# Two transformer layer pairs on one core: x tiles loaded ahead of the weights, set-up behind the norm statistics, and a scheduler told the traced DMA landings

## The chip, the cores and the metric

The kernel runs on one NeuronCore of a Trainium2 chip. The core has a matrix engine (TensorE, "PE" in the profile; its weight loads are "PEld"), a vector engine (VectorE, "DVE"), an engine for activation functions (ScalarE, "ACT"), a general engine (GpSimd, "POOL"), and a queue that issues DMAs (SyncE, "SP"). The metric is the device time of one execution in microseconds (us), as the median of several runs.

## The reference

Four steps run in sequence on `x` of 2048 tokens by 512 features in bf16: attention, feed-forward, attention, feed-forward, with the same weights both times. In the kernel the attentions are called L = 1 and L = 3.

```python
def _A_ref(x, wqkv, wo):                       # 32 heads of 16 features
    qkv = (x @ wqkv).reshape(B, S, 3, 32, 16).transpose(2, 0, 3, 1, 4)
    scores = einsum("bhqd,bhkd->bhqk", q, k) * 16 ** -0.5
    o = einsum("bhqk,bhkd->bhqd", softmax(scores), v)
    return o.transpose(0, 2, 1, 3).reshape(B, S, 512) @ wo

def _B_ref(x, w1, b1, w2, b2):                 # 512 -> 1376 -> 512
    h = gelu(layernorm(x) @ w1 + b1)
    return h @ w2 + b2

x = x + _A_ref(layernorm(x), wqkv, wo)
x = x + _B_ref(layernorm(x), w1, b1, w2, b2)
x = x + _A_ref(layernorm(x), wqkv, wo)
x = x + _B_ref(layernorm(x), w1, b1, w2, b2)
```

## The kernel before

The kernel is written as jobs (Python generators) that hand tasks to a small list scheduler when the kernel is built. The scheduler keeps a modelled clock for each engine; each operation carries a duration `dur` and, for a DMA, a latency `lat` from the end of its issue to its landing. It picks the task that can start first, ties going to the lower priority number. What comes out is one fixed order of instructions for each engine, with semaphore waits; on the chip nothing is re-ordered. The modelled times therefore decide only the order.

A tile is 128 tokens, so x has 16 tiles. A chunk `qc` is four tiles of queries, a segment is one chunk and one group of four heads (`hg`). For each segment TensorE computes scores (L1240), the softmax exponential runs on ScalarE over two or three 128x512 tiles at once (L1225), and TensorE multiplies by V (L1409). Some of the key tiles (3, 6, 9, 12, 15) may take another way: VectorE makes an approximate exponential of them with integer operations (one L1317 each, and three L1348 for each pair). The first chunk of each layer is done in two parts: for L = 1, key tiles 0 to 3 first and 4 to 15 after them, so that attention starts before all keys exist.

How a DMA was booked before:

```python
op.t0 = max(self.free[eng], self.ready(eng, reads, writes, same_ok))
if eng == "sp":
    self.free[eng] = op.t0 + dur
    op.t1 = op.t0 + dur + (2.0 if lat is None else lat)
```

The start of the kernel (shortened; `now0` puts an instruction into its stream at once, ahead of all jobs):

```python
ldx(0, 1)
ldw(1, 512)          # K weights, 512 KB
ldx(1, 2)
ldx(2, 4)
ldw(0, 0)            # Q weights
ldw(2, 1024)         # V weights
self.S_.when([("ks", 1, 1)], lambda: ldx(4, 8))
self.S_.when([("ks", 1, 3)], lambda: ldx(8, 16))     # 1 MB in one DMA
...
dve = lambda fn, reads, writes, dur=0.2: n0("dve", I(fn, reads, writes, dur))
...
dve(memset zw) ; dve(memset of a PSUM bank) ; pads("dve", 2)
dve(memset of the ones column of V) ; dve(ident) ; dve(iogt) ; dve(row16) ; dve(onesm)
dve(qbias) ; dve(ioe) ; dve(mask8) ; dve(m4) ; dve(sel memset) ; dve(sel)     # L696 to L706
```

Then each of the first four tiles goes through its norm and its projections. Norm statistics are `bn_stats` and `bn_aggr` on VectorE (L808, L809) and two small operations on GpSimd (L816, L817); the normalised tile (L821) is transposed by DMA (L968) and multiplied by the K, Q and V weights (L989). Keys are transposed by DMA straight into the key buffer `KT` (L993), queries are stored to a scratch tensor (L1020) and read back, transposed, once for each segment:

```python
def flow_q(self):                                       # one transposed read per segment
    for sg in self.segs:
        ...                                             # the very first segment uses a PE transpose
        s = yield ("get", "qraw")                       # two buffers
        yield ("keys", [("qst", L, tt) for tt in sg["toks"]])
        yield self.dma(... dma_start_transpose(self.qraw[:, s:s + 1, 0:W], self.q_scr[...]) ...)   # L1074
        self.S_.spawn(self.job_qt(sg, s), ...)
```

For the second layer the keys and values of tiles 0 to 11 pass through scratch tensors, since the buffers are still in use by the first; each head group is reloaded when its last segment of L = 1 is done and all twelve tiles are stored:

```python
def job_kload(self, hg):
    yield ("keys", [(k, 3, tt) for k in ("ks", "vs") for tt in range(12)])
    yield self.dma(... dma_start_transpose(self.KT[:, hg:hg + 1, 0:1536], self.k_scr[...]) ...)     # L1109
    yield self.dma(... dma_start(self.V[:, hg, 0:12, ...], self.v_scr[...]) ...)                    # L1111
```

What follows attention (output projection, residual, norm, feed-forward, and for L = 1 the projections of the next layer) is one block per chunk, with a priority:

```python
def post_prio(self, L, qc):
    return 0.95 if (L, qc) == (1, self.NC - 1) else 1.6 if (L, qc) == (1, self.NC - 2) else 2.2
```

The products with V have priority 1.0, scores 0.0. While TensorE would idle, the scheduler inserts matmuls of zeros (L1150, L1153) to keep its clock up.

Of the kernel before, what the change touches and what calls it, by code (L numbers as in the profile page):

```python
# [62 lines left out]
class Prog:  # L63


    def __init__(self):
        self.streams = {e: [] for e in ENGINES}
        self.last_writer = {}
        self.readers = {}
        self.ops = []  # L70
        self.dma_rr = 0
        self.free = {e: 0.0 for e in ENGINES}
        self.tiling = "full"
        self.tiles = {}
        self.drain = 0.0
        self.work = []
# [25 lines left out]
    def op(self, eng, fn, reads=(), writes=(), same_ok=(), dur=0.3, lat=None):  # L102
# [10 lines left out]
        if eng == "sp":  # L113
            self.free[eng] = op.t0 + dur
            op.t1 = op.t0 + dur + (2.0 if lat is None else lat)
# [361 lines left out]
ACCB = 6  # L477
# [10 lines left out]
class Builder:  # L488
# [169 lines left out]
    def build_startup(self):  # L658
# [5 lines left out]
        def ldx(a, b):  # L664
            n0("sp", I(lambda e: e.dma_start(self.xres[:, a:b, :], xr[:, a:b, :]), writes=[("x", tt) for tt in range(a, b)], dur=0.1))

        def ldw(k, a):
            n0("sp", I(lambda e: e.dma_start(self.wqkv[:, :, a:a + 512], wr[:, :, a:a + 512]), writes=[("wqkv", k)], dur=0.1, lat=3.0))
        ldx(0, 1)
        ldw(1, 512)  # L670
        ldx(1, 2)
        ldx(2, 4)
        ldw(0, 0)
        ldw(2, 1024)
        self.S_.when([("ks", 1, 1)], lambda: ldx(4, 8))
        self.S_.when([("ks", 1, 3)], lambda: ldx(8, 16))

        pool = lambda fn, writes, dur=0.4, reads=(): n0("pool", I(fn, reads, writes, dur))
        dve = lambda fn, reads, writes, dur=0.2: n0("dve", I(fn, reads, writes, dur))
# [10 lines left out]
        dve(lambda e: e.memset(self.zw[:, :], 0.0), [], [("zw",)], 0.2)  # L690
        dve(lambda e: e.memset(self.ps[:, ACCB, :], 0.0), [], [("ps", ACCB)], 0.6)
# [3 lines left out]
        vv = self.V[:, :, :, :, :].rearrange("p g k h d -> p (g k h) d")  # L695
        dve(lambda e: e.memset(vv[:, :, 16:17], 1.0), [], [("V", hg, kb) for hg in range(8) for kb in range(16)], 0.7)  # L696
        dve(lambda e: e.tensor_scalar(out=self.ident[:, :], in0=self.ioi, scalar1=0.0, scalar2=None, op0=ALU.is_equal), [("ioi",)], [("ident",)], 0.25)
        dve(lambda e: e.tensor_scalar(out=self.iogt[:, :], in0=self.iog[:, :], scalar1=16.0, scalar2=None, op0=ALU.is_equal), [("iog",)], [("iogt",)])
        dve(lambda e: e.tensor_reduce(out=self.row16[:, :], in_=self.iogt[:, :], axis=AX.X, op=ALU.add), [("iogt",)], [("row16",)])
        dve(lambda e: e.tensor_scalar(out=self.onesm[:, :], in0=self.row16[:, :], scalar1=-1.0, scalar2=1.0, op0=ALU.mult, op1=ALU.add), [("row16",)], [("onesm",)])  # L700
        dve(lambda e: e.tensor_scalar(out=self.qbias[:, :], in0=self.row16[:, :], scalar1=OFFSET, scalar2=None, op0=ALU.mult), [("row16",)], [("qbias",)])
        dve(lambda e: e.tensor_scalar(out=self.ioe[:, :, :], in0=self.ioe[:, :, :], scalar1=0.0, scalar2=None, op0=ALU.is_equal), [("ioe",)], [("ioe",)])
        dve(lambda e: e.tensor_reduce(out=self.mask8[:, :], in_=self.ioe[:, :, :], axis=AX.X, op=ALU.add), [("ioe",)], [("mask8",)])
        dve(lambda e: e.tensor_reduce(out=self.m4[:, :], in_=self.ioe[:, :, :].rearrange("p g h -> p h g"), axis=AX.X, op=ALU.add), [("ioe",)], [("m4",)])
        dve(lambda e: e.memset(self.sel[:, :], 0.0), [], [("sel",)])
        dve(lambda e: e.tensor_copy(out=self.sel[:, :].rearrange("p (h c) -> p h c", c=32)[:, :, 16], in_=self.m4[:, :]), [("m4",)], [("sel",)])  # L706

    def build_startup_late(self):
# [4 lines left out]
        def fills():  # L713
# [18 lines left out]
            ld = lambda fn, reads, writes: self.dma(fn, reads, writes, 4.0, 0.45, 5.0)  # L732
# [30 lines left out]
    def flow_weights(self):  # L763
# [3 lines left out]
        ld = lambda fn, writes, dur, prio: self.dma(fn, [], writes, prio, dur, 3.5)  # L767
# [982 lines left out]
```

## Time and profile before

| what | before |
|---|---|
| device time | 1646.37 us, median of 3 runs (1645.89 to 1647.75) |
| span of the profiled run | 1641.4 us, granted TensorE clock 0.994 |
| first exponential of a segment (ScalarE) | at 26.2 us |
| start of the second part of the first chunk | at 95.2 us |
| last segment of L = 1 ends (VectorE reads its sum) | at 830.7 us |
| ScalarE busy, 26.23 to 95.16 us | 60.94 of 68.93 us |
| ScalarE busy, 1060 to 1245 us | 182.85 of 185 us |

The page gives busy time of each engine. In a list by time each line has a start, a length, the engine, the source line and operation, output and input, a count and, in brackets, how long the engine stood idle before it and what ended the wait. "issue" there means that the profile shows no reason. In a table of stretches each engine has its busy time, then come the TensorE clock as a share of full speed, the mean busy share of the 16 DMA engines and the GB/s moved. The chain of waits is followed back from the last instruction of the stretch asked about.

### The profile page before, as it was taken

The page shows a single profiled execution, that of the slowest core. Times are in us where ns is not written, and L with a number is a line of the kernel's source. Part 1 is how long each engine was busy: PE and PEld are TensorE (multiplying, and loading weights), DVE is VectorE, ACT ScalarE, POOL GpSimd, SP SyncE. Part 2 cuts the span into 40 slices and gives each one's busy share as a digit, 9 for nine tenths or more (in the row PEclk, how much of TensorE's full clock was granted, in tenths as well). Part 3 has the DMA queues.
Part 4 walks back from the last instruction along what each step waited for, and adds up shares of the span by engine and source line. Part 5 has one row for each costly group of instructions (what it writes and reads, how often), then busy time and mean ns, then how long its engine had stood idle before and what let it go on. Part 6 is the DMA issues. An engine that isn't in the chain of part 4 may idle for free.

```text
span 1641.4 us, 40475 instructions
## 1 busy us (share of the span) xinstructions
PE 1555.6 (95%) x16682; PEld 504.4 (31%) x16833; DVE 1481.7 (90%) x3255; ACT 1562.2 (95%) x1383; POOL 380.0 (23%) x575
## 2 busy tenths in 40 slices
PE   8989999999999999999999998999999999999998
PEld 4222222222222222222232222322222222344444
DVE  7789999998999899989979799999899989999894
ACT  5999999999999999999999999899999999999996
POOL 4355231111310112111121134511011101222220
PEclk9999999999999999999999999999999999999999
DMA  6562000202111121112281330000000100000000
GB/s 172 110 133 61 16 8 8 43 17 65 63 24 36 31 44 57 33 29 45 84 130 45 64 84 15 18 21 8 14 11 8 21 12 8 5 19 9 23 8 14
DMA packets 181238, 66.34 MB, mean 40 GB/s; under 512 B 160859, under 2 KB 175424, under 8 KB 181056
## 3 DMA queue, kind: packets, MB, share of 16 engines
q1 hardware_dynamic: 181056, 63.75, 17.4%
q8 instruction: 135, 2.21, 0.6%
q14 instruction: 47, 0.39, 0.1%
HBM read 19.96 MB, written 15.30 MB: 21 GB/s over the span
## 4 chain that ended last, share of the span: by engine, by line
PE 49%; DVE 24%; ACT 23%; issue 3%; DMA 1%; POOL 1%; DVEq 0%; SPq 0%
ACT PT L1225 21%; PE ps L1240 19%; PE ps L1409 14%; DVE dp L1317 9%; DVE dp L1348 7%; PE ps L1574 4%; PE ps L1536 4%; PE ps L876 3%; PE ps L1503 3%; PE ps L1150 2%; DVE accT L1439 1%; DVE OT L1479 1%; ACT h L1566 1%; DVE QT L1086 1%; DVE ob L1477 1%
## 5 line engine op out<-in xcount | busy, mean ns | idle before, releaser
L1225 ACT ACTIVATE PT<-ps 128x1024 bf16<-128x1024 f32 (+1 forms) x1304 | 1486.0, 1253 | 49.4 <-PE ps L1240 43.0
L1240 PE MATMUL ps<-QT,KT 32*128 32x512 bf16 (+1 forms) x4608 | 685.6, 359 | 44.0 <-DVE dp L1317 14.9
L1317 DVE TENSOR_SCALAR dp<-ps 128x512 uint16<-128x512 f32 x869 | 583.6, 679 | 76.8 <-PE ps L1240 72.9
L1348 DVE TENSOR_SCALAR dp<-dp 128x1024 uint16<-128x1024 uint16 (+1 forms) x1323 | 515.0, 430 | 6.9 <-PE ps L1409 1.8
L1409 PE MATMUL ps<-PT,V 128*17 128x512 bf16 (+1 forms) x3624 | 489.0, 359 | 0.5 <-DVE accT L1439 0.4
L1101 POOL TENSOR_SCALAR vs<-V 128x340 bf16<-128x340 bf16 (+3 forms) x240 | 243.0, 1013 | 850.0 <-PE ps L1409 812.5
L1409 PE MATMUL ps<-dp,vs 128*17 128x512 bf16 (+1 forms) x2952 | 435.8, 358 | 1.2 <-DVE dp L1348 0.9
L1240 PEld LDWEIGHTS ps<-QT,KT 32*128 32x128 bf16 x4608 | 178.0, 91 | 574.8 <-issue 151.6
L1409 PE MATMUL ps<-dp,V 128*17 128x512 bf16 (+1 forms) x984 | 209.8, 360 | 1.7 <-DVE accT L1439 0.9
L1409 PEld LDWEIGHTS ps<-PT,V 128*17 128x17 bf16 x3624 | 116.2, 88 | 115.1 <-issue 103.6
L1409 PEld LDWEIGHTS ps<-dp,vs 128*17 128x17 bf16 x2952 | 109.7, 88 | 127.2 <-issue 108.2
L1150 PE MATMUL ps<-wqkv,zw 128*32 128x256 bf16 x2928 | 142.7, 277 | 0.3 <-DVE accT L1439 0.3
L1536 PE MATMUL ps<-yT,wf 128*128 128x512 bf16 (+3 forms) x356 | 93.7, 357 | 7.4 <-issue 4.1
L876 PE MATMUL ps<-wqkv,xnT 128*128 128x512 bf16 x299 | 84.5, 383 | 9.7 <-issue 3.2
L1150 PEld LDWEIGHTS ps<-wqkv,zw 128*32 128x32 bf16 x2928 | 73.3, 96 | 58.7 <-issue 41.6
L1439 DVE STREAM_TRANSPOSE accT<-ps 128x512 f32<-128x512 f32 (+1 forms) x88 | 57.8, 656 | 10.2 <-PE ps L1409 10.2
L1560 DVE TENSOR_SCALAR h<-ps,b1c 128x512 bf16<-128x512 f32 (+2 forms) x88 | 61.7, 701 | 4.2 <-PE ps L1536 3.8
L1503 PE MATMUL ps<-wo,OT 128*128 128x512 bf16 x209 | 60.8, 382 | 5.0 <-issue 3.7
L1409 PEld LDWEIGHTS ps<-dp,V 128*17 128x17 bf16 x984 | 51.2, 88 | 45.7 <-issue 25.4
L1479 DVE STREAM_TRANSPOSE OT<-ob 128x512 bf16<-128x512 bf16 (+1 forms) x72 | 45.8, 637 | 0.2
L1536 PEld LDWEIGHTS ps<-yT,wf 128*128 128x128 bf16 (+1 forms) x396 | 27.7, 99 | 53.5 <-issue 30.0
L1574 PE MATMUL ps<-wf,h 128*128 128x512 bf16 x143 | 40.8, 382 | 3.1 <-issue 1.7
(171 smaller groups left out, 775.2 us busy)
## 6 DMA issues: line engine op xcount, KB each, us to landing
wf<-in_B_w_dram SPq DMA_DIRECT2D x90, 128.0 KB, 2.3
q_scr<-qk SPq DMA_DIRECT2D x22, 256.0 KB, 2.1
k_scr<-qk SPq DMA_DIRECT2D x12, 256.0 KB, 2.0
out_dram<-xres SPq DMA_DIRECT2D x16, 128.0 KB, 1.7
v_scr<-vst SPq DMA_DIRECT2D x12, 136.0 KB, 2.0
V<-v_scr SPq DMA_DIRECT2D x8, 204.0 KB, 4.5
wqkv<-in_A_wqkv_dram SPq DMA_DIRECT2D x3, 512.0 KB, 5.6
q_scr<-h SPq DMA_DIRECT2D x6, 256.0 KB, 2.1
```

The source lines that it names most:

```text
L876: yield Task("pe", prio, [I(lambda e, c=c: e.matmul(self.ps[:, b, :], lhsT=xnT[:, c, :], rhs=self.wqkv[:, c, which * 512:which * 512 + 512 ...
L1101: yield Task("pool", 0.8, [I(lambda e, k=k: e.tensor_scalar(out=self.vs[:, q, k - 1, i:i + n, :], in0=src, scalar1=WSHIFT[k], scalar2=None ...
L1150: P.op("pe", lambda e, p=p: e.matmul(self.ps[p:p + 32, b, 0:w], lhsT=self.zw[:, 0:32], rhs=rhs[:, 0:w], start=st, stop=st, skip_group_chec ...
L1225: S_.submit(Task("act", 1e-5 * gi, [I(lambda e, pt=pt, n=n, b0=b0: e.activation(out=self.PT[:, pt:pt + n, :], in_=self.ps[:, b0:b0 + n, :] ...
L1240: return [I(lambda e, kb=kb, i=i: e.matmul(self.ps[:, b, i * W:(i + 1) * W], lhsT=self.KT[32 * hp:32 * hp + 32, hg, kb * 128:(kb + 1) * 12 ...
L1317: self.S_.submit(Task("dve", 0.0, [I(lambda e: e.tensor_scalar(out=self.dp[:, u, w * 512:(w + 1) * 512], in0=self.ps[:, b, :], scalar1=BIT ...
L1348: yield Task("dve", pr, [I(lambda e, k=k, v=v: e.tensor_scalar(out=self.dp[:, v, 0:N], in0=self.dp[:, u, 0:N], scalar1=float(SHIFT[k]), sc ...
L1409: ops.append((i, I(lambda e, hp=hp, v=v, ap=ap[:, i * W:(i + 1) * W], first=first and i == 0, W=W: e.matmul(self.ps[32 * hp:32 * hp + 17, ...
L1439: yield Task("dve", 0.3, [I(lambda e: e.transpose(self.accT[:, a, 0:W], self.ps[:, ACCB, 0:W]), [("ps", ACCB)], [RA], 0.17 + 0.535 * W / 5 ...
L1503: yield Task("pe", pr, [I(lambda e, hg=hg, i=i, b=b: e.matmul(self.ps[:, b, :], lhsT=self.OT[:, hg, i * 128:(i + 1) * 128], rhs=self.wo[:, ...
L1536: yield Task("pe", pr, [I(lambda e, c=c: e.matmul(self.ps[0:M, b, off:off + W], lhsT=self.w1(fc, c), rhs=self.yT[:, c, 0:W], start=(c == 0 ...
L1574: yield Task("pe", pr, [I(lambda e, fc=fc, i=i, b=b: e.matmul(self.ps[:, b, :], lhsT=self.gt(fc, i, W), rhs=self.w2(L, fc), start=(fc == 0 ...
```

## The change

No arithmetic is removed or added. The change re-orders the start, moves one load, raises a priority and gives the scheduler other numbers for DMAs:

- The x tiles 0 to 3 are loaded ahead of all weights.
- The constants that only the later steps need (L696 to L706 before) become a job of priority 1.9, so they can stand behind the norm statistics of the first tiles (1.5 to 1.8). Two places that use them now wait for the mark `consts`.
- x tiles 8 to 15 come in four loads of two tiles, after the query tile of the third segment has been asked for, instead of one load at the fourth key store. The norm jobs of these tiles wait for the marks `xld`.
- The block after chunk 2 of L = 1 gets the priority 0.95, as that of chunk 3 had.
- Engines are booked free from 0.75 us on, not from 0. A DMA may carry a size in time, and loads with a size queue up behind each other on a modelled bus. Most durations and latencies of DMAs get values closer to the landings in traces.

```diff
-        self.free = {e: 0.0 for e in ENGINES}
+        self.free = {e: 0.75 for e in ENGINES}
+        self.bus = 0.0
...
-            op.t1 = op.t0 + dur + (2.0 if lat is None else lat)
+            lat, size = lat if isinstance(lat, tuple) else (2.0 if lat is None else lat, 0.0)
+            op.t1 = op.t0 + dur + lat
+            if size:
+                self.bus = max(self.bus, op.t1 - size) + size
+                op.t1 = self.bus
...
         ldx(0, 1)
-        ldw(1, 512)
         ldx(1, 2)
         ldx(2, 4)
+        ldw(1, 512)
         ldw(0, 0)
         ldw(2, 1024)
         self.S_.when([("ks", 1, 1)], lambda: ldx(4, 8))
-        self.S_.when([("ks", 1, 3)], lambda: ldx(8, 16))
+
+        def late():
+            yield ("keys", [("qraw", 2)])
+            for a in range(8, 16, 2):
+                yield self.dma(lambda e, a=a: e.dma_start(self.xres[:, a:a + 2, :], xr[:, a:a + 2, :]), [], [("x", a), ("x", a + 1)], 1.7, 0.5, (2.24, 1.04))
+                self.S_.mark(("xld", a))
+        self.S_.spawn(late(), 1.7)
...
-        dve = lambda fn, reads, writes, dur=0.2: n0("dve", I(fn, reads, writes, dur))
+        dve = lambda fn, reads, writes, dur=0.2: Task("dve", 1.9, [I(fn, reads, writes, dur)])
...
+        def consts():
+            vv = self.V[:, :, :, :, :].rearrange("p g k h d -> p (g k h) d")
+            yield dve(lambda e: e.memset(vv[:, :, 16:17], 1.0), [], [("V", hg, kb) for hg in range(8) for kb in range(16)], 0.7)
... (the other ten constants in their old order)
+            self.S_.mark(("consts",))
+        self.S_.spawn(consts(), 1.9)
...
+        if L == 1 and tiles[0] >= 8:
+            yield ("keys", [("xld", tt) for tt in tiles[::2]])
         slot = yield ("get", "lnc")
...                                                     (transposed key store, L993 and L864)
-            yield self.dma(... dma_start_transpose(self.KT[...]) ..., prio, 2.4)
+            yield self.dma(... dma_start_transpose(self.KT[...]) ..., prio, 1.31, 1.9)
...                                                     (query store, L1020)
-            yield self.dma(... self.q_scr[0, ...] ..., prio, 0.45)
+            yield self.dma(... self.q_scr[0, ...] ..., prio, 0.45, (1.65, 1.05))
...                                                     (transposed K reload, L1109)
-                       ..., 1.4, 2.0)
+                       ..., 1.4, 1.7, 3.8)
...
+            self.S_.mark(("qraw", sg["i"]))
             self.S_.spawn(self.job_qt(sg, s), 0.5 + 0.001 * sg["i"])
...
-        return 0.95 if (L, qc) == (1, self.NC - 1) else 1.6 if (L, qc) == (1, self.NC - 2) else 2.2
+        return 0.95 if L == 1 and qc >= self.NC - 2 else 2.2
```

The other changed lines give new durations and latencies in the same manner to the norm transposes (1.25 to 1.31, landing 1.2 later), the weight loads, the stores of keys, values and queries, the reads of queries and the output stores.

## The prediction

> **What bounds the kernel now.** I read the busy line of the page first, then ScalarE in order of time, then the two places where ScalarE stands still, through VectorE, the DMA queue and the chain of waits.
>
> ```profile
> PE 1555.6 (95%) x16682; PEld 504.4 (31%) x16833; DVE 1481.7 (90%) x3255; ACT 1562.2 (95%) x1383; POOL 380.0 (23%) x575
> ```
>
> Three engines are nearly full over 1641.4 us. A change that takes no work from ScalarE can win only what ScalarE idles, 1641.4 - 1562.2 = 79 us, or shift softmax tiles to VectorE. So I ask where the 79 us lie and which of them the edits reach. ScalarE in order of time, early stretch (start, length, what, and idle time before it):
>
> ```profile
> 22.87 0.61 ACT L1027 ACTIVATE V<-ps 128x512 bf16<-128x512 f32 x1 [0.16 <-PE ps L989]
> 26.23 7.44 ACT L1225 ACTIVATE PT<-ps 128x1024 bf16<-128x1024 f32 x8 [2.75 <-PE ps L1240]
> 35.67 2.17 ACT L1225 ACTIVATE PT<-ps 128x1024 bf16<-128x1024 f32 x2 [2.01 <-PE ps L1240]
> 38.32 1.02 ACT L1225 ACTIVATE PT<-ps 128x1024 bf16<-128x1024 f32 x1 [0.47 <-PE ps L1240]
> 40.16 5.80 ACT L1225 ACTIVATE PT<-ps 128x1024 bf16<-128x1024 f32 x6 [0.82 <-PE ps L1240]
> ...
> 95.16 6.89 ACT L1225 ACTIVATE PT<-ps 128x1536 bf16<-128x1536 f32 x6 [1.50 <-PE ps L1240]
> ```
>
> The first exp starts at 26.23; before it ScalarE is busy for only 9.65 us. After the first eight exps (one segment) it waits 2.01, 0.47 and 0.82 us, and 1.50 us where part 1 of the first chunk begins (95.16). VectorE at the start:
>
> ```profile
> 2.27 0.09 DVE L689 MEMSET h<- 128x32 bf16 x1 [0.18 <-DVE h L688]
> 4.06 0.48 DVE L696 MEMSET V<- 128x512 bf16 x1 [1.71 <-issue]
> ...
> 6.16 0.17 DVE L706 CAST sel<-m 32x4 bf16<-32x4 f32 x1
> 6.24 1.27 DVE L808 BATCH_NORM_STATS2 st<-xres 128x6 f32<-128x512 bf16 x2
> ```
>
> The first norm statistic, at 6.24, waits for no data: it stands behind the set-up (L696 to L706), which runs without a break from 4.06. The first x tile was issued at 0.72 and took 2.2 us to land, so it lay ready at 2.9. The queue that issues DMAs:
>
> ```profile
> 17.69 0.58 SPq L665 DMA_DIRECT2D xres<-in_A_x_dram  x1
> ...
> 23.06 0.58 SPq L665 DMA_DIRECT2D xres<-in_A_x_dram  x1
> 23.68 1.81 SPq L1020 DMA_DIRECT2D q_scr<-h  x2
> 32.14 2.46 SPq L1074 DMA_TRANSPOSE qraw<-q_scr  x2
> ```
>
> and two pieces of the chain of waits:
>
> ```profile
> 25.05 7.01 DMA q_scr<-h
> 32.14 2.58 DMA qraw<-q_scr
> ```
>
> The last query stores are issued behind the 1 MB load of x tiles 8 to 15 (23.06) and land only at 32.06; the transposed read for the second segment starts then and lands at 34.7. That is the 2.01 us wait. The half TensorE clock that follows (0.50 from 36 to 38 us) causes the other two.
>
> The third place is the passage to the second layer (queue, then all engines in one 20 us stretch):
>
> ```profile
> 815.41 0.33 SPq L870 DMA_DIRECT2D v_scr<-vst  x1
> 815.84 5.34 SPq L1109 DMA_TRANSPOSE KT<-k_scr  x3
> ```
>
> ```profile
> 820.00:840.00 20.00, 19.43 (x242) 7.51 (x242) 11.70 (x30) 18.81 (x17) 3.50 (x7) 1.00 1.08 164
> ```
>
> All eight K and V reloads wait for the last V store at 815.41 and go in one burst until 847; DMA share is 1.08, VectorE does 11.70 of 20 us.
>
> **What the Trainium skill says.** "DMA: Bandwidth & Descriptors", Queues, rings and completion order: each DMA engine takes descriptors in the order of its ring, so a small store behind a large load shares its delay. The trace agrees: stores of 256 KB land in a median 2.1 us over the kernel, but 6.3 us behind the 1 MB load. "Perfetto Trace Analysis", DMA Instruction — HWDGE: the profiled window of a DMA instruction ends when it is issued, movement is not in it. Here 0.58 us of issue stand against 6.3 us to landing, so I count landings, not queue lines. "TensorE: Matmul & The Clock Gate", What's actually happening: about 3.4 us of too little activity halve TensorE's clock. The trace fits: TensorE is busy 0.90 us in 32 to 34 and 0.78 us in 34 to 36, then the clock is 0.50.
>
> **The change part by part.**
> *x before weights.* The same 2.05 MB move before about 9 us. x tiles 1 to 3 now go ahead of the K weights: 0.5 MB at the 360 GB/s of 3.5 to 5.5 us is an estimated 1.5 us, so they land by about 4.5 instead of at most 6.2 (issued by 2.1, 4.1 us). The K weights come about 1 us later, near 6.5. The first projection ran at 12.30, so this costs nothing.
> *Set-up behind the statistics.* 6.24 - 4.06 = 2.2 us of VectorE work leaves the front. I cannot tell whether the 1.71 us gap before 4.06 belongs to the V memset or recurs for whatever stands fifth on VectorE; I assume it recurs, so the first statistic starts near 4.2 and the first transpose near 7.4 instead of 9.43. But the work isn't gone: VectorE is busy 17.7 of the 21.7 us from 4.06 to 25.75, so 4.0 us is the whole slack, and the closing scale chain (22.15 to 25.75: reduce, transpose, power, matmul, each waiting for the last) keeps its own gaps. I take 2.5 us, between 1.5 and 3.5.
> *Late x in four pieces, behind the second prefetched query tile.* The stores should land in 3 to 4 us, the read before 28, while the first segment's exps last to about 31: the 2.01 us wait goes, and with it the slow clock and its 0.47 + 0.82. Sum 3.3 us. Its price, later statistics for tiles 8 to 15, is small: their K projections begin only near 50.
> *Part 1's start.* The key tiles 4 to 15 pass sooner, because their first transpose (34.65) stood behind the same stores. The 1.50 us at 95.16, and some of the 0.2 us waits between, shrink: 1.0 to 1.5 us, I take 1.5.
> *Priority 0.95 for layer 1's third output block.* Before, that block takes from 643 (first residual add) to 815 at priority 1.6; the fourth, at 0.95, takes from 835 to about 970. 35 us sooner dissolves the burst. VectorE's 8.3 idle us are worth 8.3 / (0.68 + 1.5 x 0.43 = 1.32) = 6 softmax tiles, each 0.46 us of ScalarE: 2.9 us, plus the 0.86 + 0.21 + 0.22 + 0.28 us waits near 830 to 848, together 4.5. Against it: ScalarE idles 5.1 us in 860 to 960, the stretch of an urgent block, and 3.3 us in 640 to 800. Over 135 and 172 us this is 6.9 against 3.5, a loss of 3.4. Net gain 1.
> *New durations and latencies in the scheduler.* They remove no instruction; they re-order the static streams everywhere. Where a direct K transpose was booked with 2.4 us of queue time it occupies 1.3. I book zero on average and a wide spread.
> Sum: 2.5 + 3.3 + 1.5 + 1 = 8.3 us; 1646.4 - 8.3 = 1638.
>
> **Rivals.** (a) *The start is VectorE-bound.* The set-up is only put off, and the gaps it should fill are too small; the first exp moves by under 1 us. For: 17.7 of 21.7 us busy. Against: it idles 0.84 us at 9.9 and 0.96 us at 12.2. Time then 1640. (b) *Re-ordering decides.* Every order after the first few us differs; one unlucky hole like the one at 166 to 172 (clock 0.50, ScalarE busy 3.75 of 6 us) gives back 2 to 3 us, and one avoided gains as much. Two or three bad ones make 1645 to 1650. For: such holes come without a DMA near them. (c) *The urgent block hurts.* If the 3.4 us loss stands and the burst's gain doesn't come, or part 1 of the second layer (ScalarE 14.59 of 20 us in 1020 to 1040) gets worse, 1644. (d) *More tiles go to VectorE.* If the smoother queue frees VectorE for 2 more tiles per segment, 1625; nothing in the stretches past 1060 (ScalarE 19.8 of 20 us) suggests much of that.
>
> **Range and chances.** The start and the store are well seen in the trace: 4 to 8 us. The passage and the order add about 6 us either way. So 1638, range 1626 to 1648. 2% is 33 us; startup and early waits hold 20 + 5 us of idle in all, and only a general collapse of the order could lose 33: 0.02 faster, 0.96 the same, 0.02 slower.
>
> **What would show it.** First statistic near 4.2, first exp at 23 to 24.5, no wait of 2 us before the ninth exp and no clock of 0.50 at 36; part 1 starting at 87 to 90 instead of 95.16; K reloads beginning near 780 in separate steps, with VectorE above 17 of 20 us there. I am wrong if the head start of some 7 us at the start of part 1 is gone by the end, or if the third block's urgency opens new waits between 640 and 780.

## The result, and the profile after

The changed kernel takes 1658.6 us in the median (1650.2 to 1663.6, six runs) against 1646.2 of the kernel before (1641.6 to 1647.8, six runs). The ratio is 1.0074, with a 95% interval of 1.0047 to 1.0101: within 2%, as predicted, but 20 us above the predicted 1638 and above the range of 1626 to 1648. The profiled execution spans 1658.0 us.

The busy line of the page after:

```profile
PE 1569.1 (95%) x16778; PEld 508.0 (31%) x16918; DVE 1484.7 (90%) x3259; ACT 1562.5 (94%) x1382; POOL 381.5 (23%) x575
```

ScalarE has the same work as before (1562.5 against 1562.2 us). So the whole difference is idle time of ScalarE: 95.5 us instead of 79. No work was added to ScalarE; it waits more.

The start. First VectorE, then the DMA queue and two pieces of the chain of waits (start, length, what):

```profile
4.04 0.48 DVE L709 MEMSET V<- 128x512 bf16 x1 [1.69 <-issue]
4.18 1.22 DVE L823 BATCH_NORM_STATS2 st<-xres 128x6 f32<-128x512 bf16 x2
```

```profile
7.26 6.23 SPq L985 DMA_TRANSPOSE yT<-dp  x4
...
30.70 2.28 SPq L685 DMA_DIRECT2D xres<-in_A_x_dram  x2
```

```profile
7.26 4.13 DMA yT<-dp
...
26.04 2.00 DMA q_scr<-h
```

The statistic starts at 4.18 instead of 6.24 and the first transpose is issued at 7.26 instead of 9.43, as predicted. But it lands 4.13 us later, at 11.39; before, it took 2.5 us and landed at 11.93. Of 2.2 us won, 0.5 are left. The query stores now land in 2.0 us instead of 7.0, since the late x pieces (L685, at 30.70) go out behind the prefetched query reads, issued at 28.19. That the statistic came at 4.18 as forecast is luck in part: I had assumed that the gap of 1.7 us recurs for whatever stands fifth on VectorE. It recurred because the memset itself stayed ahead of the statistic, and run 13 will show that the gap goes with the memset.

ScalarE in order of time:

```profile
27.61 10.19 ACT L1245 ACTIVATE PT<-ps 128x1024 bf16<-128x1024 f32 x11 [2.43 <-PE ps L1260]
...
97.73 5.97 ACT L1245 ACTIVATE PT<-ps 128x1536 bf16<-128x1536 f32 x5 [0.55 <-PE ps L1260]
```

The wait of 2.01 us ahead of the ninth exp is gone: eleven exps follow each other. But the first comes at 27.61 instead of 26.23, and part 1 of the first chunk at 97.73 instead of 95.16; I had said 23 to 24.5 and 87 to 90.

The passage to the second layer, queue and 20 us stretch (columns: TensorE, weight loads, VectorE, ScalarE, GpSimd busy, granted clock, DMA share, GB/s):

```profile
775.33 1.42 SPq L1129 DMA_TRANSPOSE KT<-k_scr  x1
...
820.00:840.00 20.00, 19.48 (x245) 6.00 (x241) 19.98 (x48) 19.86 (x18) 2.91 (x3) 1.00 0.20 39
```

This went as predicted: the reloads start at 775.33 instead of 815.84, in separate steps (the next at 778.10), and VectorE does 19.98 of 20 us where it did 11.70.

So several local effects came, and the sum went the other way. To see where, I cut both traces at the ends of the same segments (VectorE's transpose of each accumulator, L1439 before, L1459 after) and take the time in which ScalarE idles:

| stretch, in times of before, us | ScalarE idle before | ScalarE idle, changed |
|---|---|---|
| 0 to 612 | 36.9 | 40.0 |
| 612 to 812 (the third block) | 4.4 | 8.5 |
| 812 to 895 (the passage, four segments) | 4.5 | 4.6 |
| 895 to 1097 | 13.0 | 18.9 |
| 1097 to the end | 20.4 | 23.5 |

In the passage ScalarE is busy for 75.2 us instead of 78.2: the 2.9 us that I expected VectorE to take over there came. The waits, of which I expected to win some, stayed, and since ScalarE's work over the whole kernel is the same, the 3 us are given back elsewhere. The 4.1 us of new waits from 612 to 812 are a sign of being wrong that I had named, new waits between 640 and 780 under the urgent third block.

The second trace that matters is TensorE's granted clock. (1 - mean clock) times the span makes about 9 us before and 22.5 after. After, the clock is half at 12 to 15, 104 to 108, 114 to 118, 934 to 947, 1019 to 1033 and 1050 to 1057 us.

### The profile page after: what moved, and what is told of

It is laid out like the page before. It is cut to its first block, busy times and chain, and to the rows that moved or that the text cites. A ratio compares the mean times of both kernels' runs of the same rounds, so it can differ in the third digit from the quotient of the medians.

```text
span 1658.0 us, 40704 instructions
## 1 busy us (share of the span) xinstructions
PE 1569.1 (95%) x16778; PEld 508.0 (31%) x16918; DVE 1484.7 (90%) x3259; ACT 1562.5 (94%) x1382; POOL 381.5 (23%) x575
## 4 chain that ended last, share of the span: by engine, by line
PE 48%; ACT 27%; DVE 18%; DMA 3%; issue 2%; POOL 1%; SPq 0%; POOLq 0%; DVEq 0%
ACT PT L1245 25%; PE ps L1260 18%; PE ps L1429 14%; DVE dp L1337 6%; DVE dp L1368 5%; PE ps L1556 4%; PE ps L1594 4%; PE ps L893 3%; PE ps L1523 3%; PE ps L1170 2%; DMA xnT<-xn 2%; ACT h L1586 1%; DVE accT L1459 1%; DVE st L823 1%; DVE OT L1499 1%
## 5 line engine op out<-in xcount | busy, mean ns | idle before, releaser
L1170 PE MATMUL ps<-wqkv,zw 128*32 128x256 bf16 x3184 | 156.6, 279 | 2.8 <-DVE dp L1337 2.2
L1170 PEld LDWEIGHTS ps<-wqkv,zw 128*32 128x32 bf16 x3184 | 79.2, 97 | 68.0 <-issue 43.8
L1459 DVE STREAM_TRANSPOSE accT<-ps 128x512 f32<-128x512 f32 (+1 forms) x88 | 58.0, 659 | 8.8 <-PE ps L1429 8.6
L831 POOL TENSOR_SCALAR rs<-mv 128x4 f32<-128x4 f32 (+2 forms) x19 | 4.8, 254 | 190.4 <-DVE mv L824 190.1
```

Source lines behind the costliest of these rows:

```text
L1170: P.op("pe", lambda e, p=p: e.matmul(self.ps[p:p + 32, b, 0:w], lhsT=self.zw[:, 0:32], rhs=rhs[:, 0:w], start=st, stop=st, skip_group_chec ...
L1459: yield Task("dve", 0.3, [I(lambda e: e.transpose(self.accT[:, a, 0:W], self.ps[:, ACCB, 0:W]), [("ps", ACCB)], [RA], 0.17 + 0.535 * W / 5 ...
```

## The experiments

Eighteen kernels ran. The theories named in the expectations: T, the change makes transfers late (transposes behind bulk loads). O, any re-ordering of the static streams moves the time by several us, and the order before is an unusually good one. P, the urgent third block costs. Later ones (P2, F, B) are spelled out in the expectations where they come.

All of them in one table. Each ratio is to runs of before that were measured beside the kernel, so it can differ a little from the quotient of the medians. "Clock" is the median granted TensorE clock of the runs. Within each kernel the time goes with it closely: over all runs of all kernels, each taken against the mean of its own kernel, a least-squares line gives 1.24 us less for each 0.001 of clock and accounts for 88% of the variance. The last column uses that slope to put every kernel at 0.995, the clock of before. It is bookkeeping: waits of TensorE can themselves bring half clocks, and no run holds the clock fixed.

| run | us, median | ratio to before, 95% interval | clock | us at clock 0.995 |
|---|---|---|---|---|
| before, all 207 runs | 1644.0 | 1 | 0.995 | 1644 |
| changed kernel | 1658.6 | 1.0047 to 1.0101 | 0.988 | 1649 |
| 1 new DMA numbers only | 1657.3 | 1.0056 to 1.0088 | 0.993 | 1654 |
| 2 changed, with the old numbers | 1658.6 | 1.0054 to 1.0101 | 0.981 | 1642 |
| 3 priority only | 1652.2 | 1.0022 to 1.0051 | 0.992 | 1648 |
| 4 changed, V weights later | 1658.4 | 1.0047 to 1.0136 | 0.989 | 1648 |
| 5 before, overlap 0.081 | 1659.3 | 1.0065 to 1.0128 | 0.995 | 1659 |
| 6 before, hold 0.41 | 1662.7 | 1.0081 to 1.0161 | 0.991 | 1658 |
| 7 late x pieces, order kept | 1648.2 | 1.0009 to 1.0032 | 0.992 | 1645 |
| 8 start and late x, order kept | 1648.6 | 1.0011 to 1.0036 | 0.994 | 1645 |
| 9 late x pieces ahead of the reads, order kept | 1641.2 | 0.9967 to 0.9992 | 0.997 | 1643 |
| 10 before, overlap 0.081 from 640 us on | 1648.3 | 1.0017 to 1.0046 | 0.993 | 1645 |
| 11 changed, overlap 0.081 | 1662.2 | 1.0075 to 1.0150 | 0.983 | 1648 |
| 12 changed, hold 0.41 | 1660.4 | 1.0087 to 1.0148 | 0.990 | 1654 |
| 13 as 9, with start and fewer fills | 1641.7 | 0.9963 to 0.9994 | 0.996 | 1643 |
| 14 as 13, V weights later | 1643.3 | 0.9972 to 1.0001 | 0.995 | 1644 |
| 15 as 5, with priority | 1648.2 | 1.0012 to 1.0045 | 0.989 | 1641 |
| 16 as 6, with priority | 1644.1 | 0.9980 to 1.0010 | 0.993 | 1640 |
| 17 changed, old priority | 1656.6 | 1.0045 to 1.0092 | 0.986 | 1645 |
| 18 numbers and priority | 1656.6 | 1.0050 to 1.0100 | 0.991 | 1651 |

### Which part costs: each alone

**1. New DMA numbers only.** The kernel before with the new durations and latencies; start, late x load and priorities as before.

```diff
-            op.t1 = op.t0 + dur + (2.0 if lat is None else lat)
+            lat, size = lat if isinstance(lat, tuple) else (2.0 if lat is None else lat, 0.0)
+            op.t1 = op.t0 + dur + lat
+            if size:
+                self.bus = max(self.bus, op.t1 - size) + size
+                op.t1 = self.bus
 ...   # and every changed dur and lat of the diff
```

> The kernel before with nothing but the new DMA durations, latencies, the modelled bus and the 0.75 us start. Theory T (transfers): the loss comes from DMA transposes that stand behind bulk loads which the new numbers pack closer; then this kernel has the hole near 100 to 118 us (xnT transposes landing in over 4 us, clock 0.5 to 0.6) and is 4 to 8 us slower than before. Theory O (order): any re-ordering of the streams moves the time by several us in either direction; then it lies anywhere within 6 us of before, and the hole need not be there. Theory P (priority of the third block): equal to before within 2 us.

**2. The changed kernel with the old numbers.** The reverse edit on the changed kernel.

> The change with all DMA numbers put back to the old ones: x before weights, set-up behind the statistics, late x in pieces, new priority. Theory T: the first transposes still take about 4 us behind the weights (first exp near 27 us), but the hole near 100 to 118 us is gone; time within 3 us of before. Theory O: anywhere within 6 us of before. Theory P: as slow as the changed kernel, 1655 us or more.

**3. Priority only.**

```diff
-        return 0.95 if (L, qc) == (1, self.NC - 1) else 1.6 if (L, qc) == (1, self.NC - 2) else 2.2
+        return 0.95 if L == 1 and qc >= self.NC - 2 else 2.2
```

> The kernel before with only the third block's priority at 0.95; all streams are as before up to about 640 us. Theory P: at least 5 us slower than before, lost between 640 and 1060 us. Theory T: within 2 us of before, since no load moves closer to a transpose there. Theory O: within 6 us, with no fixed sign.

**4. V weights behind the first transposes**, in the changed kernel; all other streams stay as they were.

```diff
         ldw(0, 0)
-        ldw(2, 1024)
+        self.S_.when([("xt", 3)], lambda: ldw(2, 1024))    # marked when the fourth transpose is issued
```

> The changed kernel with one DMA moved: the V weights are issued after the four first transposes instead of before them; the streams of all other engines are the same as in the changed kernel. Theory T: the first transpose lands in 2.5 to 3 us instead of 4.1, the first exp comes at 25 to 26 us instead of 27.6, no half clock at 12 to 16 us, and the total falls by 1 to 4 us against the changed kernel (1658.6). Theories O and P: the start moves, but the total stays within 1 us of the changed kernel's.

Measured: each part alone is slower, the numbers by 0.72%, some 12 us, the priority by 0.37%, some 6; taking the numbers back out of the changed kernel leaves it where it was. The parts don't add up, as separate costs would, and numbers with priority (run 18 below, 1656.6) cost what the numbers cost alone. All three forecasts for run 1 missed: 2 us, 6 us and 4 to 8 us, where 12 came. Of those for run 2 only P's came, and of run 3 P's total (5.9 us); P's place came in half: ScalarE idles 5.6 us more than before in 612 to 812, but 6.9 us more behind 1097, where no block is urgent.

In run 4 the first exp came at 26.07 instead of 27.61 and no half clock at 12 to 15, but not for T's reason: its first transposes still took 3.4 to 4.3 us to land, with no V weights beside them, where T had said 2.5 to 3. What differs is that the zero matmuls ended at 10.35 instead of 9.36, so that TensorE idled 1.32 us instead of 2.38. Its total is that of the changed kernel within the noise (five runs from 1654.9 to 1665.9), so what the 1.5 us are worth at the end can't be read from it. For the start T comes back below.

### Re-ordering without meaning

**5, 6.** One constant of the scheduler's model changed by 1 to 2.5%, in the kernel before. The work is the same. **10** does the first only from 640 us of model time on, as a partner of run 3, whose streams also are those of before up to there. **11, 12** do both to the changed kernel.

```diff
-OVERLAP = {"act": 0.127, "dve": 0.08, "pool": 0.05}
+OVERLAP = {"act": 0.127, "dve": 0.081, "pool": 0.05}      # runs 5 and 11; run 10 from 640 us on
-HOLD_LATE = 0.4
+HOLD_LATE = 0.41                                           # runs 6 and 12
```

> The kernel before with one constant of the scheduler's model changed that has nothing to do with DMAs or with the change: the overlap it assumes between neighbouring VectorE instructions, 0.08 to 0.081 us. It does the same work; only the static order of the streams differs. Theory O (the order before is an unusually good one, and any other costs 5 to 12 us): 1650 to 1658 us, ratio 1.003 to 1.008. Rival T/P (the loss comes from what the change does to transfers or priorities): no reason to move, 1643 to 1647 us, ratio within 0.999 to 1.001.

> The kernel before with another such constant changed: how long TensorE's queue may delay a score matmul that is due, 0.40 to 0.41 us in the model. Same work, another order. Theory O: 1650 to 1658 us, ratio 1.003 to 1.008, and another amount than the first such run. Rival T/P: 1643 to 1647 us.

> The kernel before with the scheduler's VectorE overlap 0.08 to 0.081 us, but only once its model clock has passed 640 us: streams as before up to there, another order after it, the same work. A partner without meaning for the run that changed only the priority of layer 1's third output block, whose order also differs from 640 us on and which cost 5.9 us (1.0037). Theory O: it costs as much without any urgency, 1649 to 1657 us, ratio 1.003 to 1.008. Rival P (the urgent block itself costs): 1643 to 1646, ratio below 1.001.

> The changed kernel with the overlap constant 0.08 to 0.081 us, the partner of the run that did this to the kernel before (1659.3 us). If the changed kernel's order is an ordinary one, this moves it little either way: 1654 to 1664 us, ratio to before 1.006 to 1.012. If the change as such is worth its 4 to 8 us among ordinary orders, it comes out that much under 1659.3: 1651 to 1655. If the change as such costs, above 1662.

> The changed kernel with the hold constant 0.40 to 0.41 us, the partner of the run that did this to the kernel before (1662.7 us). Ordinary order: 1654 to 1664 us. Worth its 4 to 8 us among ordinary orders: 1655 to 1658. Costs as such: above 1665.

Measured: 15 and 19 us slower than before without any meaning in the edit, more than the change costs. From 640 us on the meaningless edit costs 0.31%, the priority 0.37%. The changed kernel moves by 2 to 4 us. Theory O holds in that the orders made anew over the whole kernel lie at 1657 to 1663 without urgency, and the changed kernel among them. It said 1650 to 1658 for runs 5 and 6: right direction, too small. In runs 5 and 6 little of it goes with the clock: by the slope they would stand at 1658 to 1659 at the clock of before.

Why are they slower? ScalarE of run 5 in 820 to 850, and its queue:

```profile
828.90 10.69 ACT L1225 ACTIVATE PT<-ps 128x1536 bf16<-128x1536 f32 x9 [8.99 <-PE ps L1240]
846.63 3.28 ACT L1225 ACTIVATE PT<-ps 128x1024 bf16<-128x1024 f32 x3 [7.04 <-PE ps L1240]
```

```profile
823.59 3.26 SPq L1109 DMA_TRANSPOSE KT<-k_scr  x2
```

There are two waits, of 9.0 and 7.0 us. The burst of K and V reloads begins when the last V store has been issued: in run 5 the store goes out at 823.11 and the first reload at 823.59, in the kernel before at 815.41 and 815.84, and the waits there are 0.86 us and less. But the first wait does not stand behind the burst. Both hang on the last tile of the third block: the scaling of the second layer's keys needs the largest key norm of all twelve tiles. On TensorE, run 5 and then before:

```profile
827.44 0.17 PE L1056 MATMUL ps<-krhs,sel 32*128 32x8 bf16 x1 [0.75 <-DVE krhs L1054]
```

```profile
822.42 0.17 PE L1056 MATMUL ps<-krhs,sel 32*128 32x8 bf16 x1
```

In run 5 the first scores follow at 828.41. The first K reload lands 4.4 us after its issue, at about 828.0, so it alone would have held them nearly as long. In the kernel before the norm is there at 822.42, and ScalarE still has exps of the first layer until 830.19; in run 5 those ended at 819.9. The second wait does stand behind the burst: a V reload is issued at 841.69, behind seven K reloads, and lands 3.5 us later, and the product with V (845.85) stands ahead of the next scores (846.18) in TensorE's fixed order. So a last tile that is 8 us later, and first-layer exps that are done 10 us earlier, cost 16 us of ScalarE here. Run 1, the numbers alone, has waits of 4.41 and 5.11 us in the same place (first reload at 826.40).

The passage is the four segments that end between 811 and 894 us before. First reload, length of these four segments, and the time in which ScalarE idles in them:

| | first reload, us | the four segments, us | ScalarE idle in them, us |
|---|---|---|---|
| before | 815.8 | 82.7 | 4.5 |
| 1 numbers only | 826.4 | 100.3 | 13.4 |
| 5, 6, 10 meaningless | 823.6, 828.5, 824.2 | 100.8, 102.9, 95.2 | 18.3, 20.8, 11.7 |
| 3 priority only | 780.6 | 79.0 | 4.3 |
| changed kernel | 775.3 | 79.8 | 4.6 |
| 15, 16 meaningless and priority | 776.4, 793.3 | 84.4, 79.6 | 5.9, 3.0 |
| 17 changed, old priority | 825.1 | 81.3 | 4.1 |
| 18 numbers and priority | 797.8 | 84.5 | 7.6 |

Over the whole kernel ScalarE idles 9.7 us more than before in run 1 and 14.4, 16.4 and 5.6 us more in runs 5, 6 and 10. So the passage makes the loss of these four. It doesn't make that of the others: in the changed kernel and in run 17 ScalarE idles no longer there than before, and over the whole kernel 16.3 and 29.0 us longer (the profile of run 17 is that of its slowest run, 1673.5 us).

### The parts with the order kept

To measure a part without re-ordering, these kernels record every instruction that the scheduler of before emits, move the few that the part concerns, and emit the list again. The order of all the rest is the same instruction by instruction.

```diff
     def op(self, eng, fn, reads=(), writes=(), same_ok=(), dur=0.3, lat=None):
+        self.log.append((eng, fn, reads, writes, tuple(same_ok), dur, lat))
 ...
         S_.run()
+        self.P = moved(self, self.P.log)     # the load of x 8 to 15 taken out, four pieces put in, and so on
```

**7. Late x pieces**, two behind the last query stores and two behind the two query reads that follow. **8.** The same, with x tiles 1 to 3 ahead of the K weights and the eleven set-up instructions of VectorE behind the first two normalisations. **9.** As 7, with all four pieces ahead of the two query reads.

> The kernel before with all five instruction streams left as they are, but for one thing in the DMA queue: the 1 MB load of x tiles 8 to 15 goes out as four 256 KB pieces, two behind the last query stores and two behind the first two transposed query reads. This is the late-x part of the change without any re-ordering. By my prediction's step: the 2.01, 0.47 and 0.82 us waits of ScalarE in the first 40 us and the half clock at 36 us go, and what is gained at 40 us lasts to the end: 1641 to 1643 us beside 1645 of before, ratio 0.998. Theory O agrees (the mechanism is right, only its sum was drowned). Rival: the gain is eaten by later waits on the way, ratio 1.000.

> As the run before it, and also the other early parts of the change, still without any re-ordering past the first 12 us: x tiles 1 to 3 ahead of the K weights in the DMA queue, and the eleven set-up instructions of VectorE behind the first two tiles' normalisation instead of ahead of the statistics. By my prediction's steps: 2.5 + 3.3 + up to 1.5 us, that is 1638 to 1640 us beside 1645, ratio 0.996, with the first exp at 23 to 24.5 us. What the traces of the changed kernel showed (transposes landing in 4.1 us behind the weights) says rather 0 to 1 us from the start: first exp at 25.5 to 26.5 us, 1641 to 1643 us, ratio 0.998.

> As the late-x run, but all four pieces stand between the last query stores and the two transposed query reads. There the second pair of pieces, behind the reads, landed only at 33.4 us, and VectorE's statistic of tile 12, which stands ahead of the second query tile's scaling in its fixed order, waited 3.2 us for them; the ninth exp came at 36.45 instead of 35.67. Here all of x should land by about 30.5, the scaling run near 32, and the ninth exp follow the eighth at 33.7 without a wait and without a half clock at 36. Theory P2 (with the order fixed, what is gained early lasts to the end): 2 to 3.3 us under before, 1640.5 to 1642 beside 1643.8, ratio 0.998 to 0.999. Rival: another wait in the same stretch takes its place, ratio 1.000.

Runs 7 and 8 missed: 1.0021 instead of 0.998, and 1.0023 with the first exp at 26.81. For run 7 the profile names the wait that took the place of the old one. VectorE and ScalarE of run 7:

```profile
33.44 0.69 DVE L808 BATCH_NORM_STATS2 st<-xres 128x6 f32<-128x512 bf16 x1 [3.21 <-DMA xres<-in_A_x_dram]
```

```profile
36.45 1.02 ACT L1225 ACTIVATE PT<-ps 128x1024 bf16<-128x1024 f32 x1 [2.76 <-PE ps L1240]
```

The query data was there in time, but in VectorE's fixed order a statistic of a later tile stands ahead of the scaling of the query, and its x piece, the third, landed only at 33.4. A DMA may be moved only as far as the consumer's own order allows. That wait accounts for 1.0 us at the first segment's end and 2.1 at the eighth; the rest of this profile's 8.2 us comes mostly at two half clocks, at 189.5 to 199.7 and 1199.8 to 1210.1, which nothing shown ties to the move. With all four pieces ahead (run 9), ScalarE reads:

```profile
26.54 7.44 ACT L1225 ACTIVATE PT<-ps 128x1024 bf16<-128x1024 f32 x8 [2.73 <-PE ps L1240]
34.36 7.89 ACT L1225 ACTIVATE PT<-ps 128x1024 bf16<-128x1024 f32 x8 [0.39 <-PE ps L1240]
```

The wait of 2.01 us is 0.39, no half clock follows, and the kernel is faster than before: 0.9979, interval 0.9967 to 0.9992, 1.8 us by the medians. At the segment ends it is 1.3 us ahead at the first and 1.2 at the eighth. Later steps come where one of the two profiles has a half clock and the other has none (-3.2 after 176, -1.6 at 858). The expected gain was 2 to 3.3 us; 1.8 by the medians lies a little below it, but the ratio gives 3.5 and its interval 1.3 to 5.4, so the size is not shown to be wrong.

**13.** As 9, with the start of run 8, and 40 of the 150 zero matmuls that keep TensorE going until the first projection taken out (they compute nothing). **14.** As 13, with the V weights behind the first transposes.

> The kernel before with its order kept, and: the late x pieces as in the run that gained (1641.2 us), x tiles ahead of the K weights, the VectorE set-up behind the first two normalisations, and 40 of the 150 zero matmuls that fill TensorE up to the first projection taken out (they compute nothing). With all 150 the same early parts moved the first exp from 26.25 to 26.81 us: the fill ran to 12.7 to 13.0 us whatever the transposes did, so an earlier statistic could not start the projection sooner. Theory F (the fill was the next wait, behind it the transposes): the fill ends near 10.9, the first projection starts at 11.4 to 11.8, first exp at 25.2 to 25.9; total 1640 to 1641, ratio 0.998. My old step (2.5 us from the start): first exp at 23.7 to 24.5, total 1638 to 1639. Rival: TensorE idles, drops to half clock at 12 to 15 us as in the changed kernel, first exp at 27 or later, total 1642 to 1644.

> As the run before it, with the V weights loaded behind the first four transposes instead of ahead of them. If the transposes issued at 7.3 us are slow because 0.5 MB of V weights move beside them, they land in 2.5 to 3 us here, the first projection starts at the end of the fill (10.9), first exp at 24.5 to 25. If they are slow at that time for another reason (they took 3.4 to 4.3 us in the changed kernel with these weights out of the way), as in the run before it: first exp at 25.2 to 25.9. Total 1639 to 1641 either way; the first exp tells, not the total.

The fill and the first projection on TensorE, in the kernel before, in run 8 and in run 13:

```profile
1.56 10.27 PE L1153 MATMUL ps<-zw 128*128 128x128 bf16 x150 [1.56 <-DVE ps L691]
12.30 7.31 PE L989 MATMUL ps<-wqkv,yT 128*128 128x512 bf16 x33 [0.47 <-DMA yT<-dp]
```

```profile
1.56 11.40 PE L1153 MATMUL ps<-zw 128*128 128x128 bf16 x150 [1.56 <-DVE ps L691]
12.80 7.50 PE L989 MATMUL ps<-wqkv,yT 128*128 128x512 bf16 x34
```

```profile
1.56 7.80 PE L1153 MATMUL ps<-zw 128*128 128x128 bf16 x110 [1.56 <-DVE ps L691]
11.73 8.89 PE L989 MATMUL ps<-wqkv,yT 128*128 128x512 bf16 x33 [2.37 <-DMA yT<-dp]
```

and of run 13 one piece of the chain, the first exp, and VectorE's set-up:

```profile
7.64 3.65 DMA yT<-dp
```

```profile
27.12 16.06 ACT L1225 ACTIVATE PT<-ps 128x1024 bf16<-128x1024 f32 x17 [2.73 <-PE ps L1240]
```

```profile
9.83 0.48 DVE L696 MEMSET V<- 128x512 bf16 x1 [1.69 <-issue]
```

In run 8 the projection stands behind the fill, which no transpose can shorten. With 110 it stands behind the transpose, which was issued at 7.64 and landed at 11.29, and TensorE, idle for 2.37 us, runs at half clock from 11.5 to 15 us. The first exp comes at 27.12, where theory F had said 25.2 to 25.9. In run 14, without V weights in the way, the projection starts at 12.24, still behind that transpose, and the first exp comes at 27.93 instead of 24.5 to 25. So of the three forecasts for the start in run 13 the rival's came (half clock, first exp at 27 or later), though not its total. The start gave at most 0.6 us at the projection (11.73 against 12.30), nothing at the first exp (26.23 before) and nothing to the total: 13 and 9 are the same (0.9978 and 0.9979). Why a transpose issued at 7.3 to 7.7 us takes 3.65 to 4.5 us to land, in every kernel that issues it so early, while one issued at 9.43 takes 2.5, stays open. The V weights are not the reason, and in run 14 the other bulk loads are in too (6 GB/s moved from 7.5 to 8.5 us).

The prediction could not tell whether the gap of 1.7 us ahead of the memset of V belonged to that instruction or to its place on VectorE. In run 13 the memset is moved to 9.83, and the gap went with it; the first statistic starts at 2.88 there. It belongs to the instruction.

### Urgency on other orders

**15, 16.** The orders of runs 5 and 6 with the priority of run 3 on top. **17.** The changed kernel with the old priorities. **18.** Run 1 with the priority of run 3.

```diff
 # 15:  OVERLAP ... 0.081 and
 # 16:  HOLD_LATE = 0.41 and
 # 18:  the new DMA numbers and
+        return 0.95 if L == 1 and qc >= self.NC - 2 else 2.2
 # 17, on the changed kernel:
-        return 0.95 if L == 1 and qc >= self.NC - 2 else 2.2
+        return 0.95 if (L, qc) == (1, self.NC - 1) else 1.6 if (L, qc) == (1, self.NC - 2) else 2.2
```

> The kernel before with the overlap constant at 0.081 (alone: 1659.3 us) and, on top, the change's priority 0.95 for layer 1's third output block. With the constant alone ScalarE loses 18 of 100 us in 800 to 900, in waits of 9.0 and 7.0 us behind the burst of K and V reloads; the kernel before loses 5 there. Theory B (the urgent block dissolves the burst, and is worth more in an order that the burst hits harder): ScalarE busy 93 to 96 us in 800 to 900, less by 3 to 6 in 600 to 800, total 1649 to 1655. Rival (what is won at 800 to 900 is lost around it, as in the changed kernel): 1656 to 1662.

> The kernel before with the hold constant at 0.41 (alone: 1662.7 us) and, on top, the change's priority of the third block. With the constant alone ScalarE is busy 79.1 of 100 us in 800 to 900. Theory B: 93 to 96 there, total 1651 to 1658. Rival: 1659 to 1666.

> The changed kernel with the priorities of before; its streams are those of the changed kernel up to some 640 us. Theory B: the burst comes back and costs ScalarE 7 to 15 us in 800 to 900, partly repaid in 600 to 800: 1658 to 1666 us. Rival: the urgency is what costs the changed kernel its time: 1650 to 1655.

> The kernel before with the new DMA numbers in the scheduler and the priority 0.95 for the third block, but its old start and its old late x load. With the numbers alone (1657.3 us) ScalarE is busy 87.1 of 100 us in 800 to 900. Theory B (the urgent block is worth what the burst costs in the order at hand): 94 to 96 there, total 1647 to 1652. Then the changed kernel (1658.6) owes the rest to what the scheduler makes of the start and the late x load. Rival (the new numbers make a worse order whatever the priority is): 1655 to 1661.

Where the burst costs much, urgency pays for itself many times: 11 us (1659.3 to 1648.2) and 19 us (1662.7 to 1644.1), to within 0.3% of before and level with it, both better than forecast. In run 16 the reloads begin at 793.27 and ScalarE goes on without a long wait:

```profile
804.99 43.41 ACT L1225 ACTIVATE PT<-ps 128x1536 bf16<-128x1536 f32 x38 [0.17 <-PE ps L1240]
```

Theory B (the burst costs, urgency cures it) holds there: ScalarE is busy for 93.3 and 96.6 us of 800 to 900, where it had said 93 to 96. It fails with the new numbers: run 18 is at 1656.6 (ScalarE busy for 88.8 us of 800 to 900, where 94 to 96 were forecast), run 1 at 1657.3, and run 17 shows that the changed kernel is no slower without urgency (1656.6). In run 18 the four segments are short (84.5 us), but the eight before them take 209.6 us against 200.2, with ScalarE busy 16.4 of 20 us and a clock of 0.74 at 800 to 820, where the reloads now fall: the hit has moved forward. In run 17 the reloads are as late as 825.14, and the four segments take 81.3 us all the same: there ScalarE has exps of the first layer until the last of its segments ends at 853.4, and its waits from 806 to 870 are 0.38 us and less. By these two traces, a late reload hurts when ScalarE has run out of first-layer work, as in run 5. I can't say what in the new numbers does it; as far as the runs go, each of these is another draw of the order.

## Why the prediction was wrong

**Late x pieces, 3.3 us.** The mechanism was right: the wait is gone in the changed kernel (eleven exps in a row) and in run 9. The size was 1.8 us there by the medians, with the interval from 1.3 to 5.4 us, which holds the forecast.

**Start, 2.5 us.** Wrong. The first statistic and the issue of the transpose moved as said; the first exp moved by +1.4 us in the changed kernel. I had followed the path statistic, transpose, projection with the landing of before (2.5 us) and taken the VectorE slack as the limit. Two waits stood right behind: the transpose issued 2 us sooner lands 0.5 us sooner, and TensorE's zero matmuls end at 11.8 us in the trace of before, only 0.47 us ahead of the projection. That line was in the trace before and I did not read it. In the changed kernel the scheduler had put in 106 fills, TensorE stood idle for 2.38 us, and the half clock that followed pushed the first exp out. Rival (a), the start bound by VectorE, was nearer in its sum, but for another reason.

**Part 1's start, 1.5 us.** It moved the other way, to 97.73 instead of 95.16. The half clock at 12 to 15 and small waits after 38 us lie ahead of it. The head start that the rest was to keep never came about.

**The urgent block, 1 us net.** Half right. VectorE took over the 2.9 us of ScalarE's work in the passage, but the waits there, from which I had expected the rest, are 4.6 us after 4.5, and the loss came where I had named it as a sign of being wrong: 4.1 us more waits in 612 to 812, 5.6 in run 3. The size of the gain was read from one order, which the burst hardly hits. In two other orders urgency is worth 11 and 19 us. So a net of 1 was no property of the change, and rival (c) not either.

**The new numbers, booked at zero on average.** This is the step that failed, with the range built on it ("about 6 us either way"). They alone cost 12.4 us, in the changed kernel their removal brings nothing, and two edits without any meaning cost 15 and 19. Rival (b) named the mechanism, but I thought of two or three small holes of 2 to 3 us; two waits that make 16 us in run 5, and half clocks of up to 13.7 us at a stretch in the changed kernel, are what came. The average of a re-ordering is not zero when the order before is a good one: of nine orders without meaning or with the numbers in them (runs 1, 2, 5, 6, 10, 11, 12, 18 and the changed kernel), none beat it. That it was picked out by tuning is likely, and no run shows it.

What the changed kernel's excess over before (1658.6 against 1644.0) consists of, then, is only known in part. By the slope of the table, its clock of 0.988 against 0.995 goes with 7 x 1.24 = 8.7 us, and 5 us are left at the same clock; that is a correlation. Its profile shows three short half clocks. The first is the start. The other two, at 104 and 114 us, follow two transposes that now stand behind loads of wo and wf, 4.71 and 4.10 us to landing, with ScalarE waits of 1.53 and 2.02 us; that the loads make them late is not shown, since the early transposes are as slow without loads beside them. The long ones, 934 to 947, 1019 to 1033 and 1050 to 1057, lie in and after the fourth block, which was urgent before too. I have not tried what would remove them.

## What to carry to other kernels

In a statically scheduled kernel, first measure what a re-ordering without meaning does: change an irrelevant constant of the model a little, two or three times. If that costs 15 us, an expected gain of 8 is not readable from the kernel as a whole; measure it with the order kept, by moving only the instructions concerned, and keep that version if it wins (here 1641 us, below both kernels). When an instruction is moved forward, read in the trace what else its consumer waits for, and how early each of these is: the gain ends at the first of them.

## What was unexpected of the hardware

The granted clock varies from run to run of the same kernel and most of the spread of its times goes with it: 1.24 us for each 0.001. It also differs from order to order: medians from 0.981 to 0.997 among kernels with the same work. The six runs of the changed kernel go from 1650.2 us at 0.995 to 1663.6 at 0.983.

The same 150 zero matmuls at the very start ended between 11.8 and 13.0 us in different kernels: they run at 21 or 22 in 2 us at first and at 40 in 2 us later, and the moment of the step differed, at about 5.2 us before and about 7 in run 9, whose instructions up to there are the same.

A memset of the ones column of V has 1.7 us ahead of it in which VectorE waits for nothing that the profile shows, wherever it stands.
